# Layer 0 in the form of layer 1: a pair of blocks by Strassen's scheme, and the next layer's norm, v and k moved into the last second product

## The chip, the cores and the metric

The kernel runs on one core of one Trainium2 chip. The metric is the device time of one execution in microseconds. The core has five engines that this text names as the profile does: PE (matrix products), DVE (element-wise work and reductions), ACT (activations and copies), POOL (a second element-wise engine) and SP (the queue that issues nearly all transfers). Each engine works through its own list of instructions in order; semaphores tie the lists together. The lists themselves are made before the run: the program is written tile by tile, and a scheduler turns it into one list for each engine, taking the instruction written first among those whose inputs and buffers it expects to be ready.

## The reference

Two equal layers over 2048 rows of 576 numbers, all in float32. Each layer is an attention part and a dense part, both with a residual:

```python
x = x + A(layernorm(x))      # q, k, v; softmax features of q and k; linear attention; wo
x = x + B(layernorm(x))      # relu(x @ w1 + b1) ** 2 @ w2 + b2,  576 -> 4608 -> 576
```

In the attention part k and v of all 2048 rows are summed to one small matrix per head before any row of the output can be made. In the dense part each row stands alone.

## The kernel before, in words

The rows are cut into four blocks of 512 (0 to 3), a block into four tiles of 128 rows. Every float32 operand is split into a high and a low piece, and a product is made of three: high by high, high by low, low by high.

A layer is a barrier (the last block's k and v, the sums, the first block's attention) and then the dense part, block by block. The order of blocks is 3, 2, 0, 1 in layer 0 and 1, 0, 3, 2 in layer 1.

`g_mlp` (L695) is the dense part of one block. It walks over 36 slices of 128 hidden features. For each it makes the first product (`hidden`, L719: 14 products of 512 columns), squares it, and adds the slice before to the output (second product, L737 and L746: 12 products of 448 columns and 3 of 512). That is 14 + 15 products of PE for each slice.

`g_pair` (L929) is the dense part of two blocks together. The first product of two blocks by two slices is a 2 by 2 product of halves, and Strassen's scheme makes it with 7 half products instead of 8. A half product (`product`, L1007) is 7 products of PE, so a pair of slices takes 49, where two `g_mlp` take 56. `split_pair` builds the seven weight operands (ACT, DVE, POOL); `g_norm_first` and `g_norm_second` build the operands of the rows from the two blocks' norms. In the first stage, `products()`, one block's second product is made at once. The other block's squared hidden values go out to memory (`hd`) and come back in a second stage that is nothing but that block's second product: 36 steps of 15 products, with `load_high` and `load_wide` two steps ahead. I call that stage the last second product.

`weave(main, other, rate)` writes two generators into one program: after each step of `main` it lets `other` go on by `rate` units, where a step of `other` costs what it yields, or 1. So `rate` and the costs set where the woven work stands in the program, and from that the scheduler makes the lists.

Before the change, layer 0 runs `g_mlp` four times. Into these are woven: the attention of the next block (`g_attend`), and, for the block whose dense part has just ended, the norm, v and k of layer 1 (`g_norm`, `g_v`, `g_k`, and `kv_tile`, which adds a tile's part to the sums). Block 3's norm, v and k run in block 2's dense part, block 2's in block 0's, and block 0's norm and k in block 1's. Block 0's v and all of block 1's come after the dense part. Layer 1 runs `g_mlp` twice, with the attention of three blocks woven into these two, and then `g_pair` for its last two blocks, with nothing woven in.

A softmax tile of k is a chain over four engines: ACT evicts the projection (L405), DVE takes maximum and minimum (L422, L423), DVE and POOL subtract (L426, L427), ACT takes exp (L428), DVE sums and inverts (L430, L431), POOL multiplies (L438), and only then can PE run that tile's `kv_tile` (L466). In the names of tiles `m_3`, `n_3`, `k_3`, `v_3` are block 3's dense part, norm, k and v; `m_p` is the pair; `m_pg` and `m_phc` are the hidden values read back and their pieces, `m_pr` and `m_ps` the raw and split slice of w2; `w_3v0h` is the high piece of the first half of v's weights.

Of the kernel before, what the change touches and what calls it, by code (L numbers as in the profile page):

```python
# [7 lines left out]
F32 = mybir.dt.float32  # L8
# [13 lines left out]
def layers_kernel(  # L22
# [160 lines left out]
    vslots = [new_slot(t, f"vslot{t}") for t in range(NT)]  # L183
    for vt in vslots:
        nc.gpsimd.memset(vt[:, : H * VW].rearrange("p (h d) -> p h d", d=VW)[:, :, 0:1], 1.0)
        nc.gpsimd.memset(vt[:, H * VW : H * VW + 32 - VW], 0.0)
# [742 lines left out]
    def g_pair(layer, blocks, x, after, name):  # L929
# [114 lines left out]
        def last_rows(b):  # L1044
# [9 lines left out]
            xs_ = []  # L1054
# [12 lines left out]
        def new_z(f):  # L1067
            tag = "hr" if f % 4 < 2 else "qk"
            return sb.tile([P, TB] if tag == "hr" else [P, D], F32, tag=tag, name=f"{name}z{f}",
                           bufs=2 if tag == "hr" else 5)[:, :TB]  # L1070

# [5 lines left out]
        def load_high(f):  # L1077
            r = sb.tile([P, D], F32, tag="qk", name=f"{name}g{f}", bufs=5)[:, :TB]
# [17 lines left out]
        def products():  # L1096
# [47 lines left out]
            last_rows(0)  # L1144
            accs[1] = [ps_a.tile([P, TB], F32, tag=tag, name=f"{name}ac{tag}") for tag in ("h", "acc0", "acc1", "acc2", "acc3")]
# [11 lines left out]
        return prelude(), products()  # L1157
# [8 lines left out]
    def g_attend(layer, b, x, raws, dst, name, behind=None, norm=None, mid=(None, None), ph=None):  # L1166

        cost = (lambda c: c) if layer else (lambda c: None)
# [6 lines left out]
        if layer:  # L1175
            yield 5.0
        if mid[0]:
            yield from mid[0]
        yield from g_out(layer, b, ph, dst, name, behind=behind and behind["last"], norm=norm, mid=mid[1],
                         costs=(cost(1.0), cost(None if norm else 3.0)))  # L1180

    def g_features(layer, raws, ph, name):
        cost = (lambda c: c) if layer else (lambda c: None)
        er = []
        yield from paced(held(g_soft(raws, er, name)), cost(5.5))
        yield from paced(held(g_phi(layer, er, ph, name, True)), cost(2.8))

    def g_queries(layer, b, x, raws, name):
        cost = (lambda c: c) if layer else (lambda c: None)
        if x is None:  # L1190
            x = unspill(b, f"{name}u")
        yield from paced(g_q(x, wpair("q", name), raws, name), cost(1.0))
# [63 lines left out]
    for layer in range(2):  # L1256
        ready, raws = barrier(layer, b, prev, x, xprev, kes, vpair)
        spare["tags"] = []
        nxt_raws = raws
        prev_rows = None  # L1260
        early = []
        operands = {}
        prelude, products = g_pair(layer, order[2:], operands, None, f"m{layer}_p")
        for i, b in enumerate(order):
            n = f"{layer}_{b}"
            if layer and i == 2:
                drain(products)
                break
            nxt = {}
            keep = {}  # L1270

            def g_back(i=i, prev_rows=prev_rows, keep=keep, nxt=nxt, nxt_raws=nxt_raws):
                if prev_rows is not None:
                    pb, rows = prev_rows
                    m = f"1_{pb}"
                    xk = {}
                    yield from g_norm(lambda t: rows[t], xk, f"n{m}")
                    if i < NB - 1:
                        spill(pb, xk)
                        vts = []  # L1280
                        yield from g_v(xk, wpair("v", f"w{m}"), vts, f"v{m}")
                        es = []
                        yield from g_k(xk, wpair("k", f"w{m}"), es, f"k{m}",
                                       then=lambda t: kv_tile(1, vts[t], es[t], f"kv{m}_{t}"))
                    else:
                        es = []
                        yield from g_k(xk, wpair("k", f"w{m}"), es, f"k{m}")
                        keep.update(x=xk, es=es, v=wpair("v", f"w{m}"))
# [24 lines left out]
            if layer == 0:  # L1313
                prev_rows = (b, rows)
# [34 lines left out]
```

## Time and profile before

| what | us |
|---|---|
| median of 3 runs (2561.92 to 2564.41) | 2562.34 |
| the profiled execution | 2562.01 |
| its span, first to last instruction | 2560.3 |
| PE busy in it | 2508.3 |
| DVE, ACT, POOL busy | 1553.0, 1271.1, 806.9 |
| layer 0, dense part: 254.4 to 1396.4 | 1142.0 |
| between the dense parts: 1396.4 to 1522.1 | 125.7 |
| layer 1, dense part: 1522.1 to 2555.7 | 1033.6 |

The time of the profiled execution is 1.7 us more than its span, and 0.3 us from the median. The granted clock of PE is 0.993 of full speed over the span. The stages are cut where PE's first product of a stage starts. A row of the table of stretches in the prediction gives, for one stretch, its length and then for each engine the busy time and, in brackets, the number of instructions. A row of a group of instructions gives line, engine, operation, what is written from what, the shapes and the count; then the busy time and the mean length of one in ns; then the idle time of the engine before them and what ended it.

### The profile page before, as it was taken

Reading aid. Unit: us, or ns where it says so; the run is one execution under the profiler, and the core shown is the slowest. Engines: PE = TensorE matmul, PEld = TensorE weight load, DVE = VectorE, ACT = ScalarE, POOL = GpSimd, SP = SyncE. Lnnn points to the kernel's source line nnn. Section 1 sums busy time; section 2 is a strip of 40 time slices with the busy share of each in tenths; the row PEclk is TensorE's granted clock in tenths of the full one; section 3 lists DMA queues with packets and bytes.
Section 4 is the critical chain, followed back from the end, with each engine's and each line's share of the span. In section 5 each row is a group of like instructions: output and inputs, shape, how many; then the busy total and the mean of one; then the engine's idle time right before and its main releaser. Section 6 shows DMA issues by size and latency. Waiting matters only on the chain. (4 is left out here: it accounts for less than half of the span.)

```text
span 2560.3 us, 41339 instructions
## 1 busy us (share of the span) xinstructions
PE 2508.3 (98%) x15282; PEld 2204.8 (86%) x15282; DVE 1553.0 (61%) x2408; ACT 1271.1 (50%) x2177; POOL 806.9 (32%) x869
## 2 busy tenths in 40 slices
PE   8998999999999999999999989999999999999999
PEld 8998888888888888888888988888888878888888
DVE  7778844456665467556434788475658565555444
ACT  4344554445554445545544435553455366666543
POOL 3444311113222132223111433132123345555322
PEclk9998999999999999999999999999999999999999
DMA  8102343354333543333433143333453344333264
GB/s 252 57 23 88 102 116 89 103 181 139 87 98 105 181 131 92 89 114 112 121 99 99 46 139 110 89 89 111 138 175 94 118 126 148 98 112 103 84 204 151
DMA packets 276757, 295.02 MB, mean 115 GB/s; under 512 B 28906, under 2 KB 206826, under 8 KB 274250
## 3 DMA queue, kind: packets, MB, share of 16 engines
q1 hardware_dynamic: 275296, 289.68, 37.7%
q8 instruction: 119, 1.95, 0.3%
q10 hardware_dynamic: 1258, 2.70, 0.3%
q14 instruction: 84, 0.69, 0.1%
HBM read 249.39 MB, written 42.89 MB: 114 GB/s over the span
## 5 line engine op out<-in xcount | busy, mean ns | idle before, releaser
L746 PE MATMUL m_0acc<-m_0s,m_0hb 128*128 128x448 f32 x864 | 199.9, 366 | 4.2 <-DVE m_0hb L729 4.2
L746 PE MATMUL m_1acc<-m_1s,m_1hb 128*128 128x448 f32 x864 | 199.3, 366 | 0.5 <-DVE m_1hb L729 0.5
L719 PE MATMUL m_0ph<-a_0nh,m_0h 128*128 128x512 f32 (+1 forms) x760 | 196.1, 386 | 3.5 <-ACT m_0hr L726 3.2
L746 PEld LDWEIGHTS m_0acc<-m_0s,m_0hb 128*128 128x128 f32 x864 | 161.7, 188 | 26.6 <-DVE m_0hb L729 6.0
L746 PEld LDWEIGHTS m_1acc<-m_1s,m_1hb 128*128 128x128 f32 x864 | 161.9, 188 | 21.4 <-DVE m_1hb L729 0.9
L719 PEld LDWEIGHTS m_0ph<-a_0nh,m_0h 128*128 128x128 f32 x760 | 136.4, 189 | 30.8 <-ACT m_0hr L726 4.4
L709 POOL TENSOR_TENSOR m_0s<-m_0r,m_0s 128x128 fp32r<-128x128 f32 x72 | 58.6, 814 | 303.9 <-ACT m_0s L705 272.6
L709 POOL TENSOR_TENSOR m_1s<-m_1r,m_1s 128x128 fp32r<-128x128 f32 x72 | 57.7, 802 | 304.1 <-ACT m_1s L705 272.2
L707 DVE TENSOR_TENSOR m_1h<-m_1r,m_1h 128x640 fp32r<-128x640 f32 x72 | 66.1, 920 | 116.0 <-ACT m_1h L704 116.0
L707 DVE TENSOR_TENSOR m_0h<-m_0r,m_0h 128x640 fp32r<-128x640 f32 x72 | 65.7, 913 | 115.8 <-ACT m_0h L704 112.7
L726 ACT ACTIVATE m_0hr<-m_0ph,b1t 128x512 f32<-128x512 f32 x72 | 49.3, 685 | 158.6 <-PE m_0ph L719 158.6
L726 ACT ACTIVATE m_1hr<-m_1ph,b1t 128x512 f32<-128x512 f32 x72 | 49.5, 687 | 153.2 <-PE m_1ph L719 153.2
L997 POOL TENSOR_TENSOR m_ps<-m_pr,m_ps 128x128 fp32r<-128x128 f32 x72 | 63.5, 882 | 184.2 <-ACT m_ps L995 160.7
L996 DVE TENSOR_TENSOR m_ps<-m_pr,m_ps 128x448 fp32r<-128x448 f32 x72 | 45.1, 627 | 102.3 <-ACT m_ps L995 102.3
L746 PE MATMUL m_2acc<-m_2s,m_2hb 128*128 128x448 f32 x432 | 99.7, 366 | 1.3 <-DVE m_2hb L729 1.3
L746 PE MATMUL m_3acc<-m_3s,m_3hb 128*128 128x448 f32 x432 | 99.5, 366 | 1.0 <-DVE m_3hb L729 1.0
L719 PE MATMUL m_1ph<-t1onh,m_1h 128*128 128x512 f32 (+1 forms) x380 | 97.9, 386 | 0.6 <-ACT t1onh L347 0.6
L719 PE MATMUL m_2ph<-a_2nh,m_2h 128*128 128x512 f32 (+1 forms) x380 | 97.2, 384 | 0.3 <-DVE m_2h L707 0.3
L719 PE MATMUL m_3ph<-t0onh,m_3h 128*128 128x512 f32 (+1 forms) x380 | 95.7, 382 | 0.1
L719 PE MATMUL m_1ph<-a_1nh,m_1h 128*128 128x512 f32 (+1 forms) x380 | 95.3, 381 | 0.0
L1036 PE MATMUL m_pacc<-m_ps,m_phb 128*128 128x448 f32 x432 | 94.0, 366 | 0.0
L746 PEld LDWEIGHTS m_2acc<-m_2s,m_2hb 128*128 128x128 f32 x432 | 80.8, 188 | 12.4 <-DVE m_2hb L729 2.2
(2076 smaller groups left out, 7114.0 us busy)
## 6 DMA issues: line engine op xcount, KB each, us to landing
m_0r<-in_B_w SPq DMA_DIRECT2D x72, 288.0 KB
m_1r<-in_B_w SPq DMA_DIRECT2D x72, 288.0 KB
m_pr<-in_B_w SPq DMA_DIRECT2D x72, 288.0 KB
m_0r<-in_B_w SPq DMA_DIRECT2D x72, 256.0 KB
m_1r<-in_B_w SPq DMA_DIRECT2D x72, 256.0 KB
m_3r<-in_B_w SPq DMA_DIRECT2D x36, 288.0 KB
m_2r<-in_B_w SPq DMA_DIRECT2D x36, 288.0 KB
m_3r<-in_B_w SPq DMA_DIRECT2D x36, 256.0 KB
```

Source lines behind the costliest of these rows:

```text
L707: nc.vector.tensor_sub(l1, r1, h1.bitcast(F32))
L709: nc.gpsimd.tensor_sub(s2[:, D + R : 2 * D], r2[:, R:], s2[:, R:D].bitcast(F32))
L719: nc.tensor.matmul(ph[:, cols], a, m, start=(k == 0), stop=(k == len(ops) - 1))
L726: nc.scalar.activation(hr, ph, AF.Relu, bias=b1t[:, f : f + 1])
L746: nc.tensor.matmul(acc[t][:, :R], a[:, rows], m, start=(f == 0 and k == 0), stop=(f == NF - 1 and k == 2))
L996: nc.vector.tensor_sub(s2[:, D : D + R], r2[:, :R], s2[:, :R].bitcast(F32))
L997: nc.gpsimd.tensor_sub(s2[:, D + R : 2 * D], r2[:, R:], s2[:, R:D].bitcast(F32))
L1036: nc.tensor.matmul(accs[b][t][:, :R], a[:, rows], m, start=(g == 0 and k == 0), stop=(g == NF - 1 and k == 2))
```

## The change

Layer 0 now has the form of layer 1. Blocks 3 and 2 run through `g_mlp`, with the attention of blocks 2, 0 and 1 woven in at the rates 3.7 and 5.0 that layer 1 has; then `g_pair` takes blocks 0 and 1. Its two stages become two generators, `products()` and `seconds()`. Into `seconds()`, block 1's last second product, are woven at a rate of 4.5: norm, v, k and the sums for block 3, the same for block 2, and norm and k for block 0. Their rows are read back from memory (`rows_of`), since their dense parts have long ended. The slots of v are made anew there (`new_slots`), because the pair has used these buffers for weights; `load_high` reads into the buffers `ft` and leaves `qk` to the raw k; one PSUM buffer (`acc4`) is added to the two for woven work.

```diff
@@ g_pair
         def load_high(f):
-            r = sb.tile([P, D], F32, tag="qk", name=f"{name}g{f}", bufs=5)[:, :TB]
+            r = sb.tile([P, TB], F32, tag="ft", name=f"{name}g{f}", bufs=4)
             nc.sync.dma_start(r, hd[f % NF])
...
             last_rows(0)
+
+        def seconds():
             accs[1] = [ps_a.tile([P, TB], F32, tag=tag, name=f"{name}ac{tag}") for tag in ("h", "acc0", "acc1", "acc2", "acc3")]
...
-        return prelude(), products()
+        return prelude(), products(), seconds()
@@ loop over the layers
-            weave(g_mlp(layer, b, ready, rows, f"m{n}", None if i else dense["turned"], then if layer and i == 1 else None),
-                  back, (3.7, 5.0)[i] if layer else 1.5 if i else 1.0)
...
+        def back_keys():
+            new_slots("vs")
+            for b in order[:3]:
+                m = f"1_{b}"
+                xk, vts, es = {}, [], []
+                yield from paced(g_norm(rows_of(b), xk, f"n{m}"), 2.7)
+                if b != order[2]:
+                    spill(b, xk)
+                    yield from paced(g_v(xk, wpair("v", f"w{m}"), vts, f"v{m}"), 1.0)
+                    yield from paced(g_k(xk, wpair("k", f"w{m}"), es, f"k{m}",
+                                         then=lambda t: kv_tile(1, vts[t], es[t], f"kv{m}_{t}")), 3.2)
+                else:
+                    yield from paced(g_k(xk, wpair("k", f"w{m}"), es, f"k{m}"), 3.2)
+                    keep.update(x=xk, es=es, v=wpair("v", f"w{m}"))
+
+        weave(g_mlp(layer, order[0], ready, [], f"m{layer}_{order[0]}", dense["turned"]), back_first(), 3.7)
+        back = back_second()
...
+        weave(g_mlp(layer, order[1], nxt, [], f"m{layer}_{order[1]}", None, then), back, 5.0)
+        drain(products)
+        spare["tags"] = ["acc4"]
+        weave(seconds, iter(()) if layer else back_keys(), 4.5)
```

The lists of the built programs show where the woven work lands. The first place is PE's list at block 3's norm. Before, inside block 2's dense part (hidden product L719, second product L746 and L737; `n_3p` are the norm's transposes):

```order
L356 MATMUL n_3p_5929<-ident,n_3e 128x128 x2
L719 MATMUL m_2ph_5947<-a_2nl,m_2h_2_5940 128x512
L719 MATMUL m_2ph_5947<-a_2nh,m_2h_2_5940 128x512 x5
L746 MATMUL m_2acc_5763<-m_2s_1_5803,m_2hb_5859 128x448 x2
L746 MATMUL m_2acc_5764<-m_2s_1_5803,m_2hb_5859 128x448 x2
L746 MATMUL m_2acc_5765<-m_2s_1_5803,m_2hb_5859 128x448 x2
L746 MATMUL m_2acc_5766<-m_2s_1_5803,m_2hb_5859 128x448 x2
L737 MATMUL m_2acc_5767<-m_2hb_5859,m_2s_1_5803 128x512 x2
```

After, in the last second product (steps 37 and 38 of the pair; lines have moved by 5, so L351 and L361 are the norm's transposes, L1041 and L1031 the second product):

```order
L351 MATMUL n_3p_12056<-ident,n_3n_12038 128x128 x4
L1041 MATMUL m_pach<-m_ps_37_11980,m_phc_11986 128x448 x3
L1041 MATMUL m_pacacc_11963<-m_ps_37_11980,m_phc_11986 128x448 x3
L1041 MATMUL m_pacacc_11964<-m_ps_37_11980,m_phc_11986 128x448 x3
L1041 MATMUL m_pacacc_11965<-m_ps_37_11980,m_phc_11986 128x448 x3
L1031 MATMUL m_pacacc_11966<-m_phc_11986,m_ps_37_11980 128x512 x3
L351 MATMUL n_3p_12102<-ident,n_3n_12051 128x128 x4
L361 MATMUL n_3p_12109<-ident,n_3e 128x128 x2
L1041 MATMUL m_pach<-m_ps_38_12006,m_phc_12012 128x448 x3
```

Before, a tile's transposes stood a whole slice (14 + 15 products) apart; now 15 products stand between them.

The second place is PE's list at the end of block 3's k: from one tile's part of the sums (`kv_3_2k`) to the last (`kv_3_3k`). Before, these are the first and last rows of that stretch, with the slice's other second products between:

```order
L466 MATMUL kv_3_2k<-k_3K2e,vslot_188 32x2x18 x32
L719 MATMUL m_2ph_6828<-a_2nh,m_2h_12_6821 128x512 x5
L719 MATMUL m_2ph_6828<-a_2nl,m_2h_12_6821 128x512 x4
L719 MATMUL m_2ph_6828<-a_2nh,m_2h_12_6821 128x512 x5
L746 MATMUL m_2acc_5763<-m_2s_11_6740,m_2hb_6844 128x448 x2
L746 MATMUL m_2acc_5764<-m_2s_11_6740,m_2hb_6844 128x448 x2
...
L737 MATMUL m_2acc_5767<-m_2hb_6844,m_2s_11_6740 128x512
L466 MATMUL kv_3_3k<-k_3K3e,vslot_189 32x2x18 x32
```

After:

```order
L471 MATMUL kv_3_2k<-k_3K2e,vs_12017 32x2x18 x32
L1041 MATMUL m_pach<-m_ps_46_12682,m_phc_12688 128x448 x3
L1041 MATMUL m_pacacc_11963<-m_ps_46_12682,m_phc_12688 128x448 x3
L1041 MATMUL m_pacacc_11964<-m_ps_46_12682,m_phc_12688 128x448 x3
L1041 MATMUL m_pacacc_11965<-m_ps_46_12682,m_phc_12688 128x448 x3
L1031 MATMUL m_pacacc_11966<-m_phc_12688,m_ps_46_12682 128x512 x3
L1041 MATMUL m_pach<-m_ps_47_12741,m_phc_12747 128x448 x3
L1041 MATMUL m_pacacc_11963<-m_ps_47_12741,m_phc_12747 128x448 x3
L1041 MATMUL m_pacacc_11964<-m_ps_47_12741,m_phc_12747 128x448 x3
L471 MATMUL kv_3_3k<-k_3K3e,vs_12018 32x2x18 x32
```

The last projection of k (tile 3) stood one slice ahead of `kv_3_2k` before, and stands one step of 15 products (step 45) ahead of it now. So between that projection and `kv_3_3k` PE had two slices of 29 products, and now has two steps and nine products, 39 in all.

The third place is ACT's list there, at the eviction of tile 3's raw k (`k_3ks`); `w_2v1h` is the high piece of the next block's v weights, whose buffer is free only when tile 3's projection has ended. After:

```order
L300 ACTIVATE w_2v0h<-w_2v0r 128x1440
L410 ACTIVATE k_3ks_12691<-k_3kp_12692 128x288
L300 ACTIVATE w_2v1h<-w_2v1r 128x1440
L410 ACTIVATE k_3ks_12691<-k_3kp_12708 128x288
L1000 ACTIVATE m_ps_47_12741<-m_pr_47_12739 128x576
L1082 ACTIVATE m_phc_12747<-m_pg_12745 128x512
L433 ACTIVATE k_3K3e<-k_3K3e 128x1152
```

Before, the weights of q (`a_0q`) stood there in the same way:

```order
L295 ACTIVATE a_0q0h<-a_0q0r 128x1440
L405 ACTIVATE k_3ks_6782<-k_3kp_6783 128x288
L295 ACTIVATE a_0q1h<-a_0q1r 128x1440
L405 ACTIVATE k_3ks_6782<-k_3kp_6799 128x288
L726 ACTIVATE m_2hr_6843<-m_2ph_6746,b1t 128x512
```

The copy of the next weights keeps its place ahead of the second eviction, and exp (L433, L428 before) now comes after a step's two copies, L1000 and L1082.

From layer 0's first hidden product to the last second product, PE's list now has 2,276 rows, as layer 1's has, and names aside the two lists agree in 99.5% of them.

102 lines of the change are left out of this document (34 added, 68 removed).

## The prediction

> **What bounds the kernel now.** I read the page's busy shares first, then a table of stretches with one row for each stage, then the waits of PE, then the groups of the two stages that the change brings together.
>
> ```profile
> span 2560.3 us, 41339 instructions
> PE 2508.3 (98%) x15282; PEld 2204.8 (86%) x15282; DVE 1553.0 (61%) x2408; ACT 1271.1 (50%) x2177; POOL 806.9 (32%) x869
> ```
>
> PE is busy in 98% of the span and no other engine in more than 61%. So time can be won in two ways only: fewer columns through PE, or less of its remaining idle time. It can be lost by making PE wait. The stages, layer 0's four dense parts first, then layer 1's four:
>
> ```profile
> core 0: us, PE busy (x) PEld busy (x) DVE busy (x) ACT busy (x) POOL busy (x), PEclk, DMA share, GB/s
> 254.40:515.30 260.90, 259.29 (x1281) 224.13 (x1282) 143.78 (x217) 131.28 (x210) 55.73 (x60) 1.00 0.36 104
> 515.30:830.30 315.00, 312.31 (x1899) 273.10 (x1899) 186.56 (x277) 155.36 (x251) 77.25 (x77) 1.00 0.40 120
> 830.30:1145.80 315.50, 312.43 (x1900) 273.19 (x1899) 187.59 (x278) 155.07 (x250) 77.23 (x77) 1.00 0.40 120
> 1145.80:1396.40 250.60, 248.79 (x1220) 215.51 (x1219) 117.21 (x170) 126.34 (x201) 51.35 (x54) 1.00 0.38 108
> 1522.10:1802.30 280.20, 277.05 (x1401) 240.95 (x1400) 189.05 (x276) 142.08 (x228) 77.47 (x74) 0.99 0.38 110
> 1802.30:2118.60 316.30, 308.94 (x1617) 267.05 (x1615) 203.13 (x323) 161.81 (x282) 103.98 (x120) 0.99 0.42 130
> 2118.60:2442.00 323.40, 321.72 (x1435) 267.36 (x1433) 169.03 (x271) 202.58 (x365) 165.53 (x214) 1.00 0.36 110
> 2442.00:2555.70 113.70, 113.70 (x545) 101.59 (x543) 55.80 (x81) 42.90 (x71) 31.05 (x35) 1.00 0.57 177
> ```
>
> Layer 0 takes 260.9 + 315.0 + 315.5 + 250.6 = 1142.0 us, layer 1 280.2 + 316.3 + 323.4 + 113.7 = 1033.6 us. Layer 1 has the attention of three blocks woven in as layer 0 has, uses Strassen's scheme, and has no norm, v and k. Its last stage is the last second product: PE without a gap, DVE at 49%.
>
> **The first product, and what moves with it.** The scheme takes 7 products of PE from each of 18 pairs of slices, 126 in all. The last second product is 432 products of 448 columns and 108 of 512, as much as 486 of 512, in 113.7 us: 0.234 us each, so 126 are worth 29.5 us on PE. That is a ceiling. Layer 1 shows what is left of it with everything that comes along (the operands' sums and splits, the trip through `hd`, the halved norms, the wait where products begin), and layer 0's list on PE becomes layer 1's almost row for row. So I don't price these edits one by one: the first three stages and the bare last one are taken from layer 1 as they stand. What has to be added is the norm, v and k that layer 1 doesn't have. Their work on PE shows undisturbed right behind layer 0's dense part, norm, v and sums of one block in the first row, k in the second:
>
> ```profile
> 1396.27:1416.89 20.62, 20.62 (x391) 19.64 (x389) 12.77 (x33) 6.78 (x13) 4.57 (x8) 1.00 0.42 131
> 1416.89:1431.89 15.00, 15.00 (x117) 15.00 (x116) 9.51 (x13) 4.40 (x9) 5.15 (x3) 1.00 0.00 1
> ```
>
> and within the first, in the timeline, the zeroing and one of four tiles' parts of the sums:
>
> ```profile
> 1403.76 0.39 PE L459 MATMUL kvp<-zero 1*128 1x288 f32 x1
> 1404.08 0.77 PE L466 MATMUL kvp<-k_0K0e,vslot 128*32 128x36 f32 x64
> ```
>
> A whole block is 20.6 + 15.0 = 35.6 us of PE. Blocks 3 and 2 are whole; block 0 has norm and k. v has as many products as k, so 20.6 less 15.0, four parts of the sums (3.1) and the zeroing (0.4) leaves 2.1 for the norm, and block 0 makes 17.1. Together 88.3 us.
>
> One wait of layer 1 has a smaller counterpart in layer 0, at the first transposes of the dense part:
>
> ```profile
> PE t1onp L346 <- DVE t1onn L331: 2.2, 1, 2.2
> PE t0onp L346 <- DVE t0onn L331: 0.6, 1, 0.6
> ```
>
> So layer 0 without new waits would be 1033.6 + 88.3 - 1.6 = 1120.3 us, which saves 21.7 of 1142.0. What follows the dense part (v of block 0, norm and k of block 1) keeps its order on all engines but for names, and is taken at no change.
>
> **What the last second product gives back.** It is the one stage without a model in the trace: a step there is 113.7 / 36 = 3.16 us of PE, where a slice of `g_mlp` has 29 products. The work to be covered is the same, the cover is half.
>
> ```profile
> L1083 DVE TENSOR_TENSOR m_phc<-m_pg,m_phc 128x512 fp32r<-128x512 f32 x34 | 32.3, 951 | 0.0
> L996 DVE TENSOR_TENSOR m_ps<-m_pr,m_ps 128x448 fp32r<-128x448 f32 x34 | 21.2, 625 | 55.7 <-ACT m_ps L995 55.7
> ...
> L316 DVE BATCH_NORM_STATS2 n_3s<-m_3x 128x6 f32<-128x288 f32 x8 | 3.3, 441 | 0.0
> L348 DVE TENSOR_TENSOR n_3l<-n_3p,n_3h 128x512 fp32r<-128x512 f32 x4 | 2.7, 687 | 0.0
> L331 DVE TENSOR_SCALAR n_3n<-m_3x,n_3m,n_3d 128x512 f32<-128x512 f32 x4 | 2.2, 548 | 2.3 <-POOL n_3d L319 2.3
> L332 DVE TENSOR_SCALAR n_3e<-m_3x,n_3m,n_3d 128x128 f32<-128x128 f32 x4 | 1.4, 344 | 0.5 <-POOL n_3d L319 0.5
> L359 DVE TENSOR_TENSOR n_3h<-n_3p,n_3h 64x256 fp32r<-64x256 f32 x2 | 0.9, 428 | 0.1
> L792 DVE TENSOR_TENSOR m_3x<-m_3acc,m_3x 128x448 f32<-128x448 f32 x4 | 2.3, 604 | 0.0
> L786 DVE TENSOR_TENSOR m_3x<-m_3py,m_3x 128x128 f32<-128x128 f32 x4 | 0.9, 280 | 0.0
> L296 DVE TENSOR_TENSOR w_3k1l<-w_3k1r,w_3k1h 128x1440 fp32r<-128x1440 f32 x1 | 1.7, 1659 | 0.2 <-ACT w_3k1h L295 0.2
> ```
>
> At its start block 3's norm comes at one tile a step, while DVE also adds block 0's result to its rows. DVE's list over steps 37 to 40 holds four pairs of `m_ps` and `m_phc` (6.3), the eight additions (3.2), statistics and scaling of two tiles (1.8 + 1.1 + 0.7), the low pieces of four (2.7 + 0.9) and two weight splits (3.3): 20.0 us. PE has four steps and the transposes to cover it, 12.6 + 2.1 = 14.7. DVE comes 5.3 us late; the last low pieces and one split (2.8) aren't needed at once, but POOL's reciprocal root stands between statistics and scaling. Bounds 0 and 6; I take 4, nearer to the list.
>
> The other place is the last tile of a block's k. The chain:
>
> ```profile
> L405 ACT ACTIVATE k_3ks<-k_3kp 128x288 f32<-128x288 f32 x8 | 3.3, 406 | 7.1 <-PE k_3kp L387 7.1
> L295 ACT ACTIVATE w_3k1h<-w_3k1r 128x1440 fp32r<-128x1440 f32 x1 | 1.4, 1412 | 0.1
> L422 DVE TENSOR_REDUCE k_3K3m<-k_3ks 128x32 f32<-128x576 f32 x1 | 0.7, 743 | 0.0
> L427 POOL TENSOR_TENSOR k_3K3e<-k_3K3m,k_3ks 128x576 f32<-128x576 f32 x1 | 1.6, 1551 | 5.1 <-DVE k_3K3m L423 5.1
> L428 ACT ACTIVATE k_3K3e<-k_3K3e 128x1152 f32<-128x1152 f32 x1 | 1.2, 1168 | 0.9 <-POOL k_3K3e L427 0.9
> L430 DVE TENSOR_REDUCE k_3K3r<-k_3K3e 128x64 f32<-128x1152 f32 x1 | 1.4, 1353 | 0.6 <-ACT k_3K3e L428 0.6
> L431 DVE RECIPROCAL k_3K3r<-k_3K3r 128x64 f32<-128x64 f32 x1 | 0.5, 539 | 0.0
> L438 POOL TENSOR_TENSOR k_3K3e<-k_3K3e,k_3K3r 128x1152 f32<-128x1152 f32 x1 | 2.2, 2158 | 1.7 <-DVE k_3K3r L431 1.7
> ```
>
> From the end of tile 3's projection: the next weights' copy on ACT (1.4), their split on DVE (1.7, while ACT evicts), two reductions (1.5), POOL's subtraction (1.6), exp (1.2), sum (1.4), inverse (0.5), POOL's multiplication (2.2): 11.5 us, and some 0.4 for the hops. On PE stand two steps (6.3), `kv_3_2k` (0.8) and nine products of 448 columns (9 x 0.205 = 1.8): 8.9. PE waits 3.0 us, in block 3 and in block 2, which has the same list; block 0 has no sums there. That is 6. The other tiles have 10.4 us or more on PE, against 9.2 for the chain without the weights (11.5 - 3.1 + 0.4 for the eviction + 0.4): nothing, near the edge.
>
> Costed at nothing: the memsets of the v slots (POOL is busy for 31 of 113.7 us in the bare stage), the hidden values' return (two steps ahead, and without a wait in layer 1 at 3.16 us a step), and the re-read rows. On SP the rows, the v and k weights and the spills stand between the prefetches of steps 37 to 62; the eight products of v at a stretch (15 us) cover them. If that cover is gone, each late prefetch holds a step.
>
> **The sum.** 2562.0 (profiled execution, 0.3 below the median of the runs) - 21.7 + 4 + 6 = 2550.3 us. I predict 2550.
>
> **Rivals.** *No give-back.* Dense parts of layer 0 with as much woven in lose no more than 3.1 us each to waits (315.5 less 312.4). If the last stage does the same, 2540 to 2545. Against it: the lists put half the PE work between the same operations.
>
> *The gain is eaten.* SP issues in order, and there the loads of weights and rows wait for buffers that DVE has yet to free, ahead of the next steps' `m_pr` and `m_pg`. Half a us on 36 steps is 18, and with half of the waits above the time is 2562 - 21.7 + 18 + 5 = 2563: no change. For it speaks the DMA share of 0.57 in the bare stage; against it, that 113.7 us at 177 GB/s are 20.1 MB, and one block's work adds at most 120 x 315.0 - 104 x 260.9, or 10.7 MB, which gives 52 MB in some 212 us at the utmost, 246 GB/s.
>
> *DVE and POOL stand in each other's way, and it gets slower.* The low piece of the hidden values usually takes DVE 0.7 us, but up to 2.6:
>
> ```profile
> L729 DVE TENSOR_TENSOR m_2hb<-m_2hr,m_2hb x36: 623/692/2641, 526.8 to 823.3; 128x512 fp32r<-128x512 f32 x36
> ```
>
> The longest is about one of POOL's multiplications (2.2) longer than the shortest. The new stage has twelve of these and twelve subtractions of 1.6 on POOL. DVE's own work is 55.8 and at most 186.6 - 143.8 = 42.8 for each of three blocks, 184 us; if each of the 24 held a DVE instruction for its whole length, 46 more, 230 us. PE has 113.7 + 88.3 = 202. DVE then sets the stage at 230, and with the start's 4 the time is 2562 - 21.7 + 28 + 4 = 2572. It turns to slower when DVE's work there passes 224 us. Against it: 42.8 already holds the collisions of a stage in which k was woven in, and q's splits.
>
> The Trainium skill's page "SBUF — State Buffer", section "Who interferes with whom", has the rule for this: a DVE instruction with two SBUF inputs and a GpSimd instruction that reads SBUF shut each other out for the whole instruction. The row above agrees with it; by the rule the collisions would come with every such pair, which is this rival's 2572, and by the rows of the second stage they are already within the 42.8.
>
> **Chances.** My forecast, 2546 to 2557, 0.5; no give-back, 0.15; gain eaten, 2557 to 2567, 0.2; DVE and POOL or another delay beyond that, 0.15. A change under 0.2%, 5 us, can hardly be told from none. Faster by more, below 2557: 0.5 + 0.15 and a small part of the third, 0.68. Within 0.2%: 0.19. Slower: 0.13. The range for 8 in 10 runs from no give-back at all (2540) into the third case's end (2566).
>
> **What the profile after would show.** Layer 0's first three stages at 280, 316 and 323 us, with 126 fewer products of the first kind. The last at 212, not 202, and PE's waits there for DVE `n_3n` or `m_phc` at the start and for POOL `k_3K3e` and `k_2K3e` at the two last tiles, some 3 us each. I am wrong if PE waits at every step there, for DMA or DVE, or if a stage before it is not layer 1's.

## The result

The changed kernel takes 2576.11 us (median of 4 runs, 2574.56 to 2576.75), the kernel before, run beside it, 2562.13 us: a ratio of 1.0052 with a 95% interval of 1.0034 to 1.0069. It is slower by about 14 us, where 12 us less were forecast. The profiled execution took 2576.0 us, with a span of 2574.2, so it stands for the median.

From the busy shares of the changed kernel:

```profile
span 2574.2 us, 41588 instructions
PE 2493.8 (97%) x15108; PEld 2185.5 (85%) x15108; DVE 1640.9 (64%) x2570; ACT 1303.3 (51%) x2293; POOL 973.6 (38%) x1101
```

PE is busy for 14.5 us less than before and the span is 13.9 us longer: PE's idle time grew from 52.0 to 80.4 us. Where it grew shows in the table of stretches. These are layer 0's four dense stages, the end of layer 0 with the start of layer 1 (125.7 us before), and layer 1's four:

```profile
core 0: us, PE busy (x) PEld busy (x) DVE busy (x) ACT busy (x) POOL busy (x), PEclk, DMA share, GB/s
254.60:534.10 279.50, 276.87 (x1400) 240.93 (x1401) 187.56 (x274) 140.52 (x227) 77.56 (x74) 0.99 0.37 109
534.10:850.30 316.20, 308.76 (x1614) 267.00 (x1613) 202.83 (x323) 161.56 (x282) 104.05 (x120) 0.99 0.42 130
850.30:1176.70 326.40, 322.01 (x1435) 267.53 (x1434) 172.38 (x281) 202.85 (x366) 166.66 (x226) 1.00 0.38 115
1176.70:1403.30 226.60, 209.27 (x1678) 191.18 (x1678) 159.58 (x224) 95.21 (x155) 80.04 (x79) 0.97 0.54 168
1403.30:1528.90 125.60, 118.59 (x1360) 115.31 (x1358) 102.32 (x177) 51.94 (x105) 53.50 (x43) 0.99 0.26 76
1528.90:1812.90 284.00, 279.20 (x1402) 242.38 (x1401) 188.64 (x276) 142.12 (x228) 77.55 (x74) 0.99 0.38 108
1812.90:2129.00 316.10, 307.52 (x1616) 265.91 (x1614) 203.01 (x323) 161.76 (x282) 103.68 (x120) 1.00 0.43 130
2129.00:2455.90 326.90, 324.11 (x1435) 267.44 (x1433) 169.03 (x271) 202.31 (x365) 165.23 (x214) 1.00 0.36 108
2455.90:2569.60 113.70, 113.70 (x545) 101.61 (x544) 55.78 (x81) 42.88 (x71) 31.07 (x35) 1.00 0.58 180
```

Layer 0's dense part takes 279.5 + 316.2 + 326.4 + 226.6 = 1148.7 us (1142.0 before, 1130.3 forecast), layer 1's 1040.7 us (1033.6 before, and silently forecast to stay). The forecast is missed by 25.7 us: 14.6 in layer 0's last second product (226.6 against 212), 3.0 in its products, 0.9 in its first stage, 7.1 in layer 1, next to nothing elsewhere.

The waits of PE in layer 0's last second product:

```profile
engine line waited for: us in total, times, longest us
PE m_pach L1041 <- DVE m_ps L1001: 5.5, 2, 4.5
PE kv_0k L471 <- POOL k_3K0e L443: 3.0, 1, 3.0
PE kv_3k L471 <- POOL k_3K3e L443: 3.0, 1, 3.0
PE kv_3k L471 <- POOL k_2K3e L443: 3.0, 1, 3.0
PE m_pach L1041 <- DVE m_phc L1083: 1.2, 3, 0.4
PE n_3p L351 <- DVE n_3n L336: 0.8, 1, 0.8
```

With one of 0.6 and one of 0.2 these are 17.3 us, where 10 were forecast. But 202.0 us of work (113.7 + 88.3) and 17.3 of waits make 219.3, not 226.6. The other 7.3 us are in PE's own busy time, 209.27 against 202.0. Four times in this stage the granted clock stood at one half for 3.41 us, which is 1.7 us of work lost each time, 6.8 in all; 0.5 us are left open. The table of stretches around the first of the four, cut at the clock's own changes:

```profile
1224.89:1228.30 3.41, 0.38 (x15) 0.13 (x17) 3.41 (x8) 0.00 (x0) 2.46 (x2) 1.00 0.52 144
1228.30:1231.71 3.41, 3.41 (x74) 3.33 (x71) 1.89 (x4) 1.83 (x3) 1.56 (x2) 0.50 0.05 20
1231.71:1235.13 3.42, 3.42 (x25) 3.35 (x24) 2.65 (x5) 1.54 (x4) 1.41 (x2) 1.00 0.28 74
```

In the first row PE waits 3.03 us for `k_3K0e`; in the second it is busy throughout, at a clock of 0.50, and does in 3.41 us the work of 1.7. The same stands behind the waits for `k_3K3e` (from 1259.0 us), `k_2K3e` (1334.1) and `m_ps` (1388.7). No stretch of before's last stage has it; its waits were of 0.5 us.

The largest wait, 4.5 us for `m_ps`, stands ahead of step 68. DVE's timeline there:

```profile
1379.17 3.61 DVE L301 TENSOR_TENSOR w_0v0l<-w_0v0r,w_0v0h 128x1440 fp32r<-128x1440 f32 x1
...
1384.69 2.61 DVE L301 TENSOR_TENSOR w_0v1l<-w_0v1r,w_0v1h 128x1440 fp32r<-128x1440 f32 x1
1387.22 0.87 DVE L1001 TENSOR_TENSOR m_ps<-m_pr,m_ps 128x448 fp32r<-128x448 f32 x1
```

Block 0's v weights, needed only after the stage, are split ahead of the operands that the next step needs, and take 3.61 and 2.61 us where such a split takes 1.66 undisturbed: POOL was multiplying beside the first and subtracting beside the second.

### The profile page after: what moved, and what is told of

Read it like the earlier page. It is cut to its first block, busy times and chain, and to the rows that moved or that the text cites. A ratio compares the mean times of both kernels' runs of the same rounds, so it can differ in the third digit from the quotient of the medians.

```text
span 2574.2 us, 41588 instructions
## 1 busy us (share of the span) xinstructions
PE 2493.8 (97%) x15108; PEld 2185.5 (85%) x15108; DVE 1640.9 (64%) x2570; ACT 1303.3 (51%) x2293; POOL 973.6 (38%) x1101
## 5 line engine op out<-in xcount | busy, mean ns | idle before, releaser
L1041 PE MATMUL m_pacc<-m_ps,m_phb 128*128 128x448 f32 x864 | 188.5, 366 | 0.0
L1041 PEld LDWEIGHTS m_pacc<-m_ps,m_phb 128*128 128x128 f32 x864 | 162.1, 188 | 18.1
L1000 ACT ACTIVATE m_ps<-m_pr 128x576 fp32r<-128x576 f32 x144 | 97.9, 680 | 142.6 <-PE m_pacacc L1031 86.1
L1041 PE MATMUL m_pacacc<-m_ps,m_phc 128*128 128x448 f32 x648 | 147.2, 370 | 0.0
L1041 PEld LDWEIGHTS m_pacacc<-m_ps,m_phc 128*128 128x128 f32 x648 | 122.9, 190 | 10.6
L751 PE MATMUL m_0acc<-m_0s,m_0hb 128*128 128x448 f32 x432 | 100.1, 366 | 2.8 <-DVE m_0hb L734 2.8
L724 PE MATMUL m_0ph<-a_0nh,m_0h 128*128 128x512 f32 (+1 forms) x380 | 98.0, 385 | 4.8 <-ACT m_0hr L731 4.7
L751 PE MATMUL m_1acc<-m_1s,m_1hb 128*128 128x448 f32 x432 | 99.4, 365 | 0.0
L751 PEld LDWEIGHTS m_1acc<-m_1s,m_1hb 128*128 128x128 f32 x432 | 81.0, 188 | 10.4
L751 PEld LDWEIGHTS m_3acc<-m_3s,m_3hb 128*128 128x128 f32 x432 | 81.0, 188 | 10.5 <-ACT m_3hb L732 0.2
L724 PEld LDWEIGHTS m_2ph<-a_2nh,m_2h 128*128 128x128 f32 x380 | 68.7, 190 | 17.3 <-ACT m_2hr L731 4.5
```

Of the source, the lines that this page charges most:

```text
L724: nc.tensor.matmul(ph[:, cols], a, m, start=(k == 0), stop=(k == len(ops) - 1))
L751: nc.tensor.matmul(acc[t][:, :R], a[:, rows], m, start=(f == 0 and k == 0), stop=(f == NF - 1 and k == 2))
L1000: nc.scalar.activation(s2[:, :D], r2, AF.Copy)
L1041: nc.tensor.matmul(accs[b][t][:, :R], a[:, rows], m, start=(g == 0 and k == 0), stop=(g == NF - 1 and k == 2))
```

## The experiments

The theory from here: PE is held by a few waits in the last stage, each of which costs its own length and, if long enough, 1.7 us more at half clock. The first rival: the half clock comes for another reason, and only the waits count. The second: the waits follow from the work's density, and move on when one is taken away. All diffs are against the changed kernel.

### Moving what PE waits for

The sums one tile further behind, in `back_keys`:

```diff
-                    yield from paced(g_k(..., then=lambda t: kv_tile(1, vts[t], es[t], f"kv{m}_{t}")), 3.2)
+                    for i, _ in enumerate(g_k(xk, wpair("k", f"w{m}"), es, f"k{m}")):
+                        if i % 2:
+                            t = i // 2
+                            sums_due.append((vts[t], es[t], f"kv{m}_{t}"))
+                            if t > 1:
+                                kv_tile(1, *sums_due.pop(0))
+                        yield 3.2
```

(and `sums_due` is emptied at the next block's first norm steps). The split of block 0's v weights later:

```diff
-                    keep.update(x=xk, es=es, v=wpair("v", f"w{m}"))
+                    yield 9.0
+                    with tc.issue_after(dense["high"].ins):    # load_high's last subtraction
+                        keep.update(x=xk, es=es, v=wpair("v", f"w{m}"))
```

And both edits.

> The sums of each tile of k are put one tile further behind (the last two tiles' among the next block's norm), so that PE no longer stands before kv_3_0k, kv_3_3k and kv_2_3k for POOL (3.03 + 3.01 + 3.00 us in the changed kernel). Theory 'half clock' (a wait of PE of more than some 2.3 us is followed by one 3.41 us stretch at half the granted clock, which costs 1.7 us more): three waits of 3.0 and three stretches of 1.7 go, 14.1 us, from 2576.1 to 2562, and no stretch below 0.99 stands at these three places. Rival 'waits only' (the stretches at half clock come for another reason): 9.0 us go, 2567, and stretches remain in the stage. Rival 'moved on' (something else is late next): 2571 or more.

> The split of block 0's v weights, which stood on DVE ahead of step 68's operands, is held behind step 70's hidden values. If that split makes the wait of 4.52 us at step 68: half clock, 4.5 + 1.7 = 6.2 us less, 2570; waits only, 4.5 less, 2571.6. If the wait is k's last tile's (its two reductions and its subtraction stay ahead of step 68's operands): the wait stays above 2.3 us and the time within 2 us of 2576. If block 0's v then comes late behind the dense part: no gain either, and the wait appears before v1_prev.

> Both moves together. Half clock: 14.1 + 6.2 = 20.3 us less than 2576.1, 2556, which is faster than the kernel before by 6 us; layer 0's last second product 206 us instead of 226.6. Waits only: 13.5 less, 2562.6, the same as before. Moved on: above 2567.

Measured: sums later 2578.1 us, v later 2568.2, both 2576.4 (against before 1.0065, 1.0022 and 1.0058, each +-0.0014 or less). The v split was worth 7.9 us by the medians, a little over the 6.2 forecast; its profiled execution was the slowest of its eight (2574.3 us), so its stages don't show the gain. The sums went the wrong way: the wait for `k_3K0e` was gone, but PE waited longer for the last tiles. In block 2 the scheduler had put these sums 8.7 us behind the projection, the wait not counted (10.9 in the changed kernel); in block 3 the chain from projection to sums took 17.6 us (12.8). Waits of PE in the last stage with the sums later:

```profile
PE m_pach L1041 <- DVE m_ps L1001: 7.4, 3, 4.9
PE kv_3k L471 <- POOL k_2K3e L443: 7.1, 1, 7.1
PE kv_3k L471 <- POOL k_3K3e L443: 4.2, 1, 4.2
```

"Moved on" was right here. The run doesn't tell whether the sums could have been held without waits; the next set does.

### A ladder of waits

In layer 1's last second product, which has no wait, ahead of every fourth step from the 5th to the 29th:

```diff
+        def pause(f, copies):
+            hh = high[f][0]
+            a, b = wtile(f"{name}za{f}"), wtile(f"{name}zb{f}")
+            d = sb.tile([P, TB], F32, tag="hr", name=f"{name}zd{f}", bufs=2)
+            nc.tensor.matmul(a, hh[:, :P], hh, start=True, stop=True)
+            nc.scalar.activation(d, a, AF.Copy)
+            for _ in range(copies - 1):
+                nc.scalar.activation(d, d, AF.Copy)
+            return nc.tensor.transpose(b[:, :P], d[:, :P], ident)
```

with 1 to 7 copies, and the step's products held behind the transpose.

> The changed kernel with seven waits put into layer 1's last second product, which has none (113.7 us, PE without a gap): ahead of steps 5, 9, 13 ... 29 PE makes one extra product, ACT copies it 1, 2, 3 ... 7 times, and PE turns a part of the copy before it goes on. So PE waits some 1 us at the first place and some 0.6 us more at each further one, up to 4 to 5 us. Half clock: from the place on where the wait passes some 2.3 us (the third or fourth), each is followed by a stretch of 3.41 us at 0.50, none before it, and the stage grows by the waits and 1.7 us for each such stretch: 20 us of waits + 4 x 1.7. Rival: the stretches come from load or chance; none stand here, or they stand at other places, and the stage grows by the waits alone.

The waits came out at 1.60, 2.26, 2.92, 3.58, 4.25, 4.89 and 5.57 us. Stretches of the run, cut at the clock's changes, the one with the wait and the one behind it, for the first three; then the whole stage:

```profile
2471.31:2474.72 3.41, 1.81 (x10) 1.47 (x9) 1.49 (x2) 1.69 (x3) 0.89 (x1) 1.00 0.56 174
2474.72:2478.13 3.41, 3.41 (x18) 3.06 (x18) 0.71 (x2) 1.21 (x2) 0.66 (x1) 1.00 0.38 132
2485.00:2488.41 3.41, 1.29 (x6) 0.74 (x4) 1.67 (x3) 2.23 (x4) 0.90 (x1) 1.00 0.49 163
2488.41:2491.82 3.41, 3.27 (x10) 2.93 (x11) 0.00 (x0) 0.08 (x1) 0.00 (x0) 0.50 0.53 163
2502.03:2505.44 3.41, 1.11 (x5) 0.56 (x4) 1.49 (x3) 2.38 (x5) 0.89 (x1) 1.00 0.50 163
2505.44:2508.85 3.41, 2.79 (x8) 2.53 (x9) 0.00 (x0) 0.57 (x1) 0.00 (x0) 0.50 0.53 168
...
2455.50:2610.70 155.20, 130.13 (x559) 113.49 (x557) 55.62 (x81) 59.44 (x99) 31.03 (x35) 0.89 0.41 131
```

This is one execution. The wait of 1.60 leaves the clock at 1; those of 2.26 and 2.92 are followed by one stretch of 3.41 us at half, the four longer ones by 6.83 us, where one stretch had been expected for each. The stage grew by 41.5 us: 25.1 of waits, some 2 for the added products, and the rest, some 14 us, PE's work at half clock. Half clock is shown as an effect of the waits; the rival that it comes for another reason is out.

### Holding the sums, and the splits at the start

Held: `kv_tile` for the last two tiles of a block is emitted at the first and the fourth step of the next norm, behind the last product of the newest step of the second product (with v later). Start: the two splits of block 0's q weights behind the last scaling of the preceding norm (with v later). Then all three.

```diff
+                    if sums_due and i in (0, 3):
+                        with tc.issue_after(dense["step"].ins):
+                            kv_tile(1, *sums_due.pop(0))
...
-            mid = (g_queries(layer, order[2], None, later, m), ...)
+            mid = (held(g_queries(layer, order[2], None, later, m), ("scaled",)), ...)
```

> The later split of block 0's v weights (2568.2 us with it alone) and, beside it, the sums of the last two tiles of blocks 3 and 2 held behind a step of the second product: kv_3_3k and kv_2_3k stand at least two steps behind their tile, where putting them one tile later by the planner's own estimate had left them waits of 4.2 and 7.1 us. Half clock: three waits of 3.0 and their stretches (1.7 each) go, 14.1 us, and DVE's lateness at block 2's norm (2.1 and 1.2 us in the run with the sums later) stays: 2568.2 - 14.1 + 3.3 = 2557. Rival 'DVE bounds that stretch': the waits come back before m_ps or m_phc in full, 2565 to 2569.

> The later split of v (2568.2 us alone) and, beside it, the two splits of block 0's q weights held behind the last scaling of the norm at the start of layer 0's dense part, where they stand in the kernel before. If they make the waits there (1.37 + 2.28 us and one stretch at half clock, against 0.6 us and none before): 3.05 + 1.7 = 4.7 us less, 2563.5, and the first stage falls from 279.5 to 275. If something else makes them, or q then comes late: 2568.

> All three: the sums held, v's split and q's splits later. If the parts add: 2557 - 4.7 = 2552, some 10 us or 0.4% faster than the kernel before. If the half clock isn't the reason, the waits alone: 2568.2 - 9 + 3.3 - 3 = 2559.5, 0.1% faster at most.

Measured: sums held 2573.3 us (2568.5 to 2575.6), start 2566.2 (ratio to before 1.0017, 1.0008 to 1.0025), all three 2567.4. The start was worth 2.0 us by the medians, not 4.7, and that lies within the spread of the two kernels' runs. Its waits did fall to 0.62 + 0.61 us and the half clock there went, and layer 1's first stage, which the edit touches too, went from 284.0 to 282.0. Holding the sums gave nothing: 5.1 us more than v later alone. The waits for POOL are gone, and DVE's are in their place; waits of PE with the sums held, a stretch of this run, and two rows of DVE's timeline in it:

```profile
PE m_pach L1042 <- DVE m_ps L1001: 5.1, 4, 2.1
...
PE m_pach L1042 <- DVE m_phc L1084: 2.7, 4, 1.5
PE n_2p L351 <- DVE n_0m L322: 1.8, 1, 1.8
...
1240.00:1264.00 24.00, 18.62 (x264) 15.41 (x265) 23.87 (x30) 10.17 (x16) 10.02 (x9) 0.93 0.67 201
...
1241.39 2.64 DVE L1084 TENSOR_TENSOR m_phc<-m_pg,m_phc 128x512 fp32r<-128x512 f32 x1
...
1254.64 2.57 DVE L1001 TENSOR_TENSOR m_ps<-m_pr,m_ps 128x448 fp32r<-128x448 f32 x1
```

Around block 3's last tiles and block 2's norm DVE is busy for 23.87 of 24 us, with single subtractions of 2.6 us where they take 0.6 to 0.7 elsewhere. In the changed kernel DVE is busy for 20.7 of the same 24 us, with PE's wait for `kv_3k` among them; that this wait gave DVE the time to catch up is a reading that no run tests. "DVE bounds that stretch" was right, and the sum of 2557 wrong.

### Spreading the norm

All three edits, with the weave's costs changed: a norm step 6.0 (or 4.4) in place of 2.7, a k step 1.5 (or 2.2) in place of 3.2, 4.1 units a step in place of 4.5.

```diff
-                    yield 2.7
+                    yield 6.0
...
-        weave(seconds, iter(()) if layer else back_keys(), 4.5)
+        weave(seconds, iter(()) if layer else back_keys(), 4.1)
```

> All three moves (2567.4 us, where DVE's lateness at block 2's and block 0's norm had taken the place of the sums' waits), and the weave's costs so that a block's norm is spread over some 7 steps of the second product in place of 3, k over 3 in place of 5, and the whole over all 35 steps. Theory 'DVE is late where the norm stands' (the sum of its waits there some 9 us, two or three stretches at half clock): those go, the stage falls from 222.4 to some 210 and the time to 2556. Rival 'DVE or the chain of k bounds the stage as a whole': the waits come back among k's tiles, which now stand closer, and the time stays above 2564.

> The same, halfway: a norm over some 5.4 steps, k over 4.3. First theory: most of the waits at the norm go, 2556 to 2560; if the crowding of k's tiles weighs more, this is the better of the two. Rival: 2564 or more, as with all three moves alone.

Measured: 2572.6 and 2569.0 us; the last stage 227.3 and 223.5, against 222.4 with all three edits alone. The waits at the norm went as expected, and others came among the tiles of k, now closer together. With the wide norm:

```profile
PE k_3kp L392 <- DVE w_3k0l L301: 5.2, 1, 5.2
PE kv_2k L471 <- POOL k_2K2e L443: 3.6, 1, 3.6
PE kv_2k L471 <- POOL k_3K2e L443: 3.3, 1, 3.3
PE m_pacacc L1031 <- ACT m_phc L1083: 3.2, 1, 3.2
```

The rival was right: with these costs the waits only moved.

For one thing in DVE's list no edit was made. In the changed kernel, at the last tile of block 3's k:

```profile
1245.72 1.64 DVE L301 TENSOR_TENSOR w_2v0l<-w_2v0r,w_2v0h 128x1440 fp32r<-128x1440 f32 x1
1247.29 1.65 DVE L301 TENSOR_TENSOR w_2v1l<-w_2v1r,w_2v1h 128x1440 fp32r<-128x1440 f32 x1
1248.86 0.74 DVE L427 TENSOR_REDUCE k_3K3m<-k_3ks 128x32 f32<-128x576 f32 x1
```

Raw k was evicted at 1246.31, so its first reduction starts 2.5 us late, behind the splits of block 2's v weights, which PE first reads at 1274.5. At block 2's last tile the splits of block 0's k weights stand in the same way (1322.38 to 1325.60), and PE first needs them after 1349. No run holds these four splits back as the v split of block 0 was held, so it is open whether the waits of 3.0 us at `kv_3k` could be shortened that way.

### Collisions or cover

With v and q later (2566.2 us): k's multiplication on DVE in place of POOL; block 3's norm, v and k in the stage ahead of Strassen's products, between its two attentions; both.

```diff
-        nc.gpsimd.tensor_mul(e3, e3, r2.unsqueeze(2).to_broadcast([P, 2 * H, DH]))
+        (nc.vector if name.startswith("k1_") else nc.gpsimd).tensor_mul(e3, e3, ...)
...
             yield from g_attend(layer, order[2], None, None, operands, f"a{layer}_{order[2]}", None,
                                 g_norm_first, ph=early)
+            if layer == 0:
+                yield from back_keys(order[:1], "vr")
...
-        weave(g_mlp(layer, order[1], nxt, ...), back, 5.0)
+        weave(g_mlp(layer, order[1], nxt, ...), back, 5.0 if layer else 6.2)
-        weave(seconds, iter(()) if layer else back_keys(), 4.5)
+        weave(seconds, iter(()) if layer else back_keys(order[1:3], "vs"), 3.2)
```

> Both splits later (2566.2 us), and the multiplication of k's features by the inverse sums, 1152 columns for each of twelve tiles of the woven k and four behind the dense part, on DVE in place of POOL (2.2 to 2.4 us there; the sum over the same columns takes DVE 1.35). Theory 'DVE and POOL hold each other up': DVE's operand splits beside these multiplications lose their long forms (m_ps 1.6 to 2.6 us in place of 0.62, the split of weights 3.6 in place of 1.66), k's chain is 1 us shorter, and the waits before kv_0k and kv_3k fall from 3.0 to some 2 us or less; the stage loses 3 x 1 + 3 x 1.7 = 8 us: 2558. Rival 'DVE's own sum of work bounds it': 12 x 1.35 = 16 us more on DVE turn up as waits before m_ps and m_phc: 2570 or more.

> Both splits later, and block 3's norm, v and k woven into the block-wise first and second product ahead of Strassen's, where a step has 29 products to cover them and not 15, as in the kernel before. Theory 'half the cover makes the waits': the last stage loses block 3's 35.6 us of PE and its waits (0.83 + 3.19 + 3.00 us and two stretches of 1.7): 221.5 - 35.6 - 10.4 = 175.5; the stage that takes it in grows by 35.6 and some 1 to 3 us of waits; together 2566.2 - 10.4 + 2 = 2558. Rival 'waits come with the work wherever it stands': the gain in the last stage comes back in the other, 2564 to 2568.

> Both together. If cover and collisions are both causes: 2558 less what the one leaves of the other, 2552 to 2556, faster than the kernel before by 0.2 to 0.4%. If DVE's own work bounds the last stage: 2562 or more.

Measured: 2567.3, 2568.4 and 2567.3 us; none differs from 2566.2 by more than the runs' spread. The stretches tell more. First the last stage with v and q later, then with the multiplication on DVE:

```profile
1172.80:1394.30 221.50, 206.43 (x1677) 188.56 (x1676) 159.58 (x228) 94.97 (x155) 78.33 (x79) 0.98 0.54 170
```

```profile
1172.70:1394.30 221.60, 207.59 (x1678) 189.81 (x1677) 161.07 (x240) 94.42 (x155) 50.39 (x67) 0.98 0.54 170
...
L443 DVE TENSOR_TENSOR k_3K0e<-k_3K0e,k_3K0r x1: 1340/1340/1340, 1222.2 to 1222.2; 128x1152 f32<-128x1152 f32 x1
```

DVE took over twelve multiplications of 1.34 to 1.36 us, 16.2 us, and its busy time grew by 1.5. So some 14.7 us of DVE's time in the stage had been POOL's multiplications holding it up. Taking that away changed neither the waits at `kv_0k` and `kv_3k` (2.9, 3.6 and 3.6 us, now for DVE) nor the time: neither "collisions" nor "DVE's own sum" sets the end alone; what still stands at those three places is k's chain, longer than the products put between. And with block 3's work in the stage before:

```profile
532.10:897.00 364.90, 350.05 (x2115) 304.59 (x2115) 236.22 (x375) 179.37 (x313) 121.52 (x135) 0.98 0.43 131
1221.60:1397.90 176.30, 170.41 (x1177) 153.96 (x1177) 128.70 (x171) 76.28 (x124) 63.29 (x63) 0.98 0.58 179
```

The last stage lost 45.2 us, as the theory of cover had it (175.5 forecast, 176.3 measured). The other stage gained 48.6 for 35.6 us of work: it has waits of 4.8 us (for DVE's `m_2h`, new) and 3.8 (for ACT's `m_2hr`, 2.3 with v and q later), and 17.1 us at half clock (none with v and q later). PE's busy time grew by 42.4 us, 6.8 more than the work. The rival, that waits come with the work wherever it stands, describes the time.

Two more, with both edits and 5.6 or 7.0 units a slice in the stage ahead of Strassen's:

```diff
-        weave(g_mlp(layer, order[1], nxt, ...), back, 5.0 if layer else 6.2)
+        weave(g_mlp(layer, order[1], nxt, ...), back, 5.0 if layer else 7.0)
```

> The kernel with block 3's norm, v and k in the stage before Strassen's and k's multiplication on DVE (2567.3 us; that stage 365.4, with waits of 4.8 and 3.8 us, and 171.8 in the last), with the weave of that stage slower: 5.6 units a slice in place of 6.2, so that the attentions and block 3's k fill it to its end. If its waits come from crowding: some 5 to 8 us less with their stretches at half clock, 2560 to 2562. If they come from what has to be done when the next stage begins, and now comes later still: 2570 or more.

> The same with 7.0 units a slice: the woven work is done earlier and the stage's last slices stand bare. If the waits come from crowding: 3 to 6 us more, 2571 to 2573. If from the stage's end: less, 2560 to 2564.

Measured: 2568.8 and 2566.1 us. Both lie between what the two theories gave, so they don't tell them apart. With 7.0 the ratio to before is 1.0015 (1.0006 to 1.0025): no order tried gets below the kernel before.

### Layer 1's slower products

PE, DVE, ACT and POOL have the same rows in the same order in both kernels from the end of layer 1's norm on. Yet a pair of slices in its products takes 17.88 us (17.75 before, 17.76 in layer 0 of the changed kernel; medians of 17 distances), each product a little longer, and there are waits for `m_pz` that before doesn't have. What is known to differ is where the buffers lie and, in SP's list, the place of a few `m_pg` reads. Two of the differences in the buffers undone: the load's buffers, and the PSUM banks that two products take in turn (here with v and q later).

```diff
-            r = sb.tile([P, TB], F32, tag="ft", name=f"{name}g{f}", bufs=4)
+            if layer:
+                r = sb.tile([P, D], F32, tag="qk", name=f"{name}g{f}", bufs=5)[:, :TB]
...
+                done = product(k, by, "a12", "b21", True)
+                if layer and k == 0:
+                    with tc.issue_after(done.ins):
+                        nc.tensor.transpose(other[:, :P], ident, ident)    # other: a "w" buffer taken ahead of by
```

> The changed kernel with layer 1's hidden values for the second block loaded into the buffers they had before (those of q and k, five, not those of the features, four). Every matmul of layer 1's products takes a little longer in the changed kernel (a pair of slices 17.84 to 17.88 us, 17.76 before and in layer 0). If where those buffers lie is the reason: a pair at 17.76 again and layer 1's products and last stage some 2 us shorter, 2574. If not: 17.85 and 2576.

> The kernel with both splits later (v's and q's, 2566.2 us), and in layer 1's products one extra use of a PSUM buffer, so that the products that take turns in two banks lie the other way round, as in the kernel before. PE, DVE, ACT and POOL have the same lists in layer 1 in both kernels, yet a pair of slices there takes 17.85 to 17.88 us after the change and 17.75 before it. If the banks are the reason: 17.76 again, and layer 1's products 2 us shorter. If not: 17.85, and the cause stays open.

Measured: 2576.5 and 2569.0 us, a pair at 17.85 and 17.84. Neither is the cause; it stays open.

## Why the prediction was wrong

- **"The first three stages and the bare last one are taken from layer 1 as they stand."** Right in the main: 279.5, 316.2 and 326.4 against 278.6, 316.3 and 323.4. The term of -1.6 for a shorter wait at the start did not come: the wait at `t0onp` was 2.3 us, where layer 1 has 2.2 before the change and 0.6 was taken. That wait depends on what else stands in DVE's list there: the two splits of block 0's q weights had been put ahead of the last norm, PE waited 1.4 + 2.3 us, and the run with these splits later has 0.6 + 0.6 in their place. The 3.0 us in the products are mostly three waits for DVE's `m_pz` (2.8 us), which weren't forecast; no run was made for them alone.
- **The work moved, 88.3 us.** Right to 0.5 us: 202.0 with the bare stage, against 209.27 busy, of which some 6.8 are the half clock.
- **"At its start ... I take 4."** Too much: 0.6 + 0.8.
- **"PE waits 3.0 us, in block 3 and in block 2."** The waits are right to a tenth, 3.01 and 3.00, but in part by luck. From the end of the projection to the sums the chain takes 12.8 us in block 3 and 13.9 in block 2, where 11.9 was forecast, and what PE has meanwhile, short waits for DVE included, is 9.8 and 10.9, where 8.9 was. Two weight splits, not one, stand on DVE ahead of the reductions.
- **"The other tiles ...: nothing, near the edge."** Wrong for the first tile of block 3: 3.0 us. There block 2's norm stands in DVE's list between the links of the chain. The first reduction starts 1.9 us after raw k is evicted, and the sum 1.5 us after exp, because DVE waits 0.97 us for POOL's `n_2d` in between. The chain takes 13.0 us, where 9.2 was forecast. A chain that ends near the edge should have had a price.
- **The v weights of block 0.** "What follows the dense part keeps its order" let the split of these weights through without a price. It came into the dense part, 4.5 us of waiting at step 68, and was worth 7.9 us when moved.
- **The half clock.** Missing altogether: some 6.8 us in the last stage. The sum priced a wait at its length, while before's trace already had the pattern, a 2.2 us wait at `t1onp` with a half-clock stretch behind it.
- **Layer 1 taken as unchanged.** Wrong by 7.1 us: 3.8 at its start, where the wait at `t1onp` is 3.9 us (2.2 before) and is followed by 6.83 us at half clock (3.41 before), since the scheduler put 14 hidden products ahead of it in place of 28; 3.5 in its products, open.
- **The rivals.** DVE's busy time in the last stage was 159.6 us, not 230, so DVE did not become the bound by its sum; the collisions were there (14.7 us by the run with k on DVE), but taking these away did not change the time. They lengthened the two splits ahead of step 68, where PE waited 4.5 us; how much of that wait they made, no run shows. No wait of PE there was for a late prefetch through SP. The forecast of 2572 for this rival lies near the 2576 measured, but not by its mechanism. No single rival made the kernel slower: several waits did, each of 3 to 5 us, with what the clock added.

The step that failed is "what the last second product gives back": 24.6 us in place of 10. Of these, 17.3 are waits: 1.4 at the start (4 forecast), 6.0 at the two last tiles of k (6 forecast) and 9.9 that were not forecast, above all 4.5 at step 68 and 3.0 at the first tile of block 3. Some 6.8 are the half clock behind four of the waits, which had no term. Together with the stages taken over as they stood it turns the sign: 21.7 saved, less 24.6 here, 7.1 in layer 1, 3.0 in layer 0's products and 0.9 in its first stage, is 13.9 us lost, the growth of the span. With v and q later the stage is 221.5 and the kernel 2566.2, still 4 us above the kernel before.

## What to carry to other kernels

In these traces a wait of PE has two prices, its length and, from about 2 us on, half of the next 3.4 us of work; count both before weaving work into a stage that had none. Saved products are worth what the cover around them allows: here 126 products (29.5 us) were saved, but the woven work moved into a stage with half the products per step to hide the same chains. Holding back block 0's v split gained 7.9 us; no other reordering tried gained more than the runs' spread. Work that a scheduler may place freely, such as a weight split for a later stage, has to be looked up in the new order on every engine, not assumed to stay.

## What the runs showed of the hardware

**The clock is decided in fixed windows.** In all eighteen traces each stretch at a granted clock of 0.50 is one to four times 3.413 us long (the last is cut by the end of the program), and starts on a grid of that step that stays fixed through the run and lies differently in each. I cut every trace at its grid, took PE's idle time in each window that ran at full clock (from 100 us on), and looked at the next window:

```
PE idle in the window, us    windows    next one at half clock
under 1.4                   12460         0
1.4 to 1.7                    110         5
1.7 to 1.9                     38        17
1.9 to 2.0                     12        11
2.0 and more                  120       120
```

So somewhat more than half a window of idling is enough. A wait of 2 to 3 us costs 1.7 us more only if enough of it falls into one window, which depends on where the grid lies in that run; with v and q later, one of three waits of 3.0 us had no half-clock stretch behind it. This may also be why the woven kernels spread more from run to run (2564 to 2571 us with v and q later); that wasn't tested. The Trainium skill's page "TensorE: Matmul & The Clock Gate", section "What's actually happening", has the free-running window of 3413 ns, and the traces agree (steps of 3.413 us). The same section of the Trainium skill's page gives half clock after a whole idle window, some 3.4 us, and there the traces differ: 2.0 us in one window sufficed 120 times out of 120.

**Handing DVE's work to POOL saved DVE almost nothing.** Twelve multiplications take POOL 2.2 to 2.5 us each and DVE 1.35; on POOL they lengthened DVE's other instructions in the last stage by 14.7 us, nearly the 16.2 us that DVE needs to do them itself.

**The same lists on four engines can run 0.5 to 0.7% slower:** layer 1's pairs at 17.84 to 17.88 us in place of 17.75. Other buffers for the load and other PSUM banks did not change it.
